# A fused attention and softplus layer on one core: the branch to the general path moved ahead of the last two units, and matmul steps unmixed

## The chip, the cores and the metric

The kernel runs on 1 core of one Trainium2 chip. The metric is device microseconds of one execution. Before the change three runs gave 687.23, 687.34 and 687.76 us; the median is 687.34 us.

## What is computed

The reference computes windowed attention with four sink keys (4 batches, 8 heads, 768 positions, head size 64, window 128), lays the heads side by side into x (3072 tokens x 512), and puts x through a layer with a softplus between two weight matrices:

```python
scores = scale * np.matmul(q, k.transpose(0, 1, 3, 2))
scores = np.where(is_sink | in_window, scores, -1000000000.0)
a = np.exp(scores - max); a = a / (a.sum + 1e-09)
x = (a @ v).transpose(0, 2, 1, 3).reshape(B * S, H * D)
h = x @ w_in                                      # 512 -> 2048
g = np.maximum(h, 0.0) + np.log1p(np.exp(-np.abs(h)))
return (g @ w_out).astype(np.float32)             # 2048 -> 512
```

The result has float32 accuracy. Each operand of the wide products is therefore kept as a rounded high part and a low remainder (`xh`/`xl`, `gh`/`gl`, and two planes of each weight), and a product is three matmuls: high by high, low by high, high by low.

## The kernel before

**Tiles.** The 3072 tokens are cut into 12 chunks of 256 (`CT`). The hidden width of 2048 is cut into 8 units of 256 (`FP`). For unit s of a chunk, `up(s)` makes `h` (128 partitions x 2 x 256) with 24 matmuls of 256 columns (line 574). `softplus(s)` runs Abs, Exp and Ln on ACT (lines 582 to 584). `gate(s)` adds the maximum on DVE (line 590) and rounds the result to `gh`, mostly on POOL (line 63). `residue(s)` makes `gl` on DVE (line 67). `down(s)` adds unit s into the two accumulators of the chunk with 12 matmuls of 512 columns (line 617); after unit 7 `store` copies both accumulators to SBUF, one on ACT and one on DVE, and SP stores them (line 629).

**Order.** `_fast` writes the order of all engines by hand. A string `START` gives the first stretch; then a loop over i runs one step per head, and each letter of a string in `STEADY` issues one piece of work for a unit or a head that lies a fixed distance from i. A step holds `up` of unit i-8, `softplus` and `gate` of that unit, `residue` of unit i-9, `down` of unit i-10 (units are counted through all chunks, 0 to 95), and the attention of one head: scores S (lines 263, 264), values V (lines 438, 444), and the work of the other engines between them. From i = 19 on (`MIXED`) the letters M and m issue `up` and `down` mixed: two up matmuls, one down matmul, and so on. For that `up` and `down` are generators that yield after each matmul, and `mixed` draws from them. Attention ends at i = 96; from then on a step is `up`, `down` and the work between. Step 103 has `up` of unit 95 and `down` of unit 93; steps 104 and 105 have the `down` of units 94 and 95 alone.

**The branch.** The fast path is valid only for some inputs. `_fast_flag` (line 817, issued at i = 100) reduces what was seen to one integer. When `_fast` is through, `values_load` (line 1003) loads it into a register on all five engines, and `tc.If(ok < 1)` (line 1004) enters `_general`, a complete second computation, when it is 0. With these inputs it is 1, so every engine jumps over the code of `_general`. Where the branch isn't taken, each engine runs a short block, also line 1004, that waits until the engine's own work so far is done and then raises the engine's semaphore by as much as `_general` would have. Later waits thus count the same on both paths. Before the change only the end of the program (line 1037) stands behind that block.

The two lines on which this hangs:

```python
        ok = nc.values_load(c.flag[:1, :1], min_val=0, max_val=1)
        with tc.If(ok < 1):
            _general(c)
```

Of the kernel before, what the change touches and what calls it, by code (L numbers as in the profile page):

```python
# [22 lines left out]
P = 128  # L23
# [446 lines left out]

def _weight_dma(c, s, k, half):

    src = c.a["w"][s, k, :, half * WH : (half + 1) * WH]
    tag = f"{WTAG[k]}{s}{half}"
    r = c.wp.tile([P, 4 * WH if c.w64 else 2 * WH], I16 if c.w64 else F32, tag=tag, name=f"{tag}r")
# [48 lines left out]
def _weight_high(c, e, eng):  # L528

    s, k, half = e  # L530
    n = (4, 2)[k]
    tag = f"{WTAG[k]}{s}{half}"
    c.w[e] = c.wp.tile([P, 2, n // 2, WC // n], F32R, tag=tag, name=tag)
    w, x = _weight_parts(c, e)
    _copy(c.nc, eng, w[:, 0], x)
# [20 lines left out]
class _Moe:  # L556
# [7 lines left out]
    def up(self, s):  # L564
        c, nc = self.c, self.c.nc
        xh, xl = c.x[self.chunk]
        if c.ps_h is None:
            c.ps_h = c.follow("ps_h")
        h = c.ps_h.tile([P, 2, CT], F32, tag="h", name=f"h{self.chunk}_{s}")
        prods = [(e, cc, j) for cc in range(4) for e in ("hh", "lh", "hl") for j in range(2)]  # L570
        for k, (e, cc, j) in enumerate(prods):
            wt = c.w[s, 0, cc // 2][:, "hl".index(e[0]), cc % 2, j * P : (j + 1) * P]
            x = (xh if e[1] == "h" else xl)[:, cc]
            nc.tensor.matmul(h[:, j], wt, x, start=k == 0, stop=k >= len(prods) - 2, skip_group_check=True)  # L574
            yield
        self.h[s] = h
# [25 lines left out]
    def down(self, s, *js):  # L602
        c, nc = self.c, self.c.nc
        if s == 0 and js[0] == 0:
            self.acc = [c.ps_acc.tile([P, DM], F32, tag=f"acc{t}", name=f"acc{self.chunk}_{t}") for t in range(CH)]
        gh, gl = self.g[s]
        prods = [(j, t, x, e) for x, e in ((gh, 0), (gh, 1), (gl, 0)) for j in js for t in range(CH)]
        if len(js) == 1:
            prods.sort(key=lambda p: p[1])
        else:  # L610
            prods[: 4 * len(js)] = sorted(prods[: 4 * len(js)], key=lambda p: p[:2])
        last = s == FP - 1 and js[-1] == 1
        for k, (j, t, x, e) in enumerate(prods):
            start = s == j == 0 and t not in [p[1] for p in prods[:k]]
            stop = last and t not in [p[1] for p in prods[k + 1 :]]
            w = c.w[s, 1, j][:, e, 0]
            nc.tensor.matmul(  # L617
                self.acc[t][:], x[:, j, t * P : t * P + P], w, start=start, stop=stop, skip_group_check=True
            )
            yield  # L620
        if last:
            self.store()

    def store(self):
        c, nc = self.c, self.c.nc
        for t, acc in enumerate(self.acc):
            o = c.stg.tile([P, DM], F32, tag="stg", name=f"o{self.chunk}_{t}")
            _copy(nc, c.E["out"][t], o[:], acc[:])
            nc.sync.dma_start(c.out[bass.ds(self.row + t * P, P), :], o[:])


def _fast(c):
# [57 lines left out]

    def products(i, name, k, *args):
        m, s = divmod(i, H)
        if not 0 <= i < n * H:
            return iter(())
        while any(e[:2] == (s, k) for _, e in todo["l"]):
            stage("l")(i)
        return getattr(moe[m], name)(s, *args)

    def dense(*args):
        return lambda i: list(products(i, *args))  # L700

    def mixed(rest):
        def run(i):
            done, live, rounds = object(), True, 6
            if not rest:
                c.mix = products(i, "up", 0), products(i - lag, "down", 1, 0, 1)
                if (i - lag) % H == 0:
                    rounds = 0
                    for _ in range(12):
                        next(c.mix[0], None)  # L710
            up, down = c.mix
            while live and (rest or rounds):
                rounds -= 1
                got = [next(p, done) for p in (up, up, down)]
                live = any(g is not done for g in got)

        return run
# [17 lines left out]
    def idle(k):  # L735
# [39 lines left out]
    with c.tc.manual_schedule():  # L775
# [15 lines left out]
        for i in range(2 * H + 1, (n + 1) * H + lag + 1):  # L791
            for part in "JjGLx" + c.STEADY[i >= c.MIXED][i % H == 0]:
                run, ahead = parts[part]
                run(i + ahead)
            if i >= 2 * H + lag and i % 2 == 0 and checks:
                _weight_check(c, *checks.pop(0))
            if i == n * H + lag:
                for e in checks:
                    _weight_check(c, *e)
                _fast_signs(c)  # L800
            if i == n * H + 2 * lag:
                _fast_flag(c)


# [54 lines left out]
def _general_masks(c):  # L859
# [7 lines left out]
    for i in range(NB):  # L867
# [58 lines left out]
def _general(c):  # L926

    tc, nc = c.tc, c.nc
    with ExitStack() as st:
        pool = lambda n, bufs: st.enter_context(tc.tile_pool(name=n, bufs=bufs))  # L930
        psum = lambda n, bufs: st.enter_context(tc.tile_pool(name=n, bufs=bufs, space=bass.MemoryType.PSUM))
        c.stg, c.gp, c.xp, c.mp = pool("gstg", 2), pool("gp", 1), pool("gxp", 1), pool("gmp", 1)
        c.ps_acc, c.ps_h, c.gs, c.gt, c.gx = psum("gacc", 1), psum("gh", 1), psum("gs", 1), psum("gt", 1), psum("gx", 1)
        _general_weights(c)
        keep = _general_masks(c)
        with tc.For_i(0, B, 1) as b:
            for n in range(NCH):
                xh, xl = c.x[n] = [c.xp.tile([P, 4, CT], F32R, tag=f"x{e}", name=f"gx{e}{n}") for e in "hl"]
                for h in range(H):
                    if h % 2 == 0:  # L940
                        xt = c.gx.tile([P, CT], F32, name=f"g_x{n}_{h}", tag="g_x")
                    _general_head(c, b, n, h, keep, xt)
                    if h % 2 == 1:
                        _copy(nc, "A", xh[:, h // 2], xt[:])
                        _sub(nc, "V", xl[:, h // 2], xt[:], xh[:, h // 2])
                m = _Moe(c, n)
                m.row = b * S + n * CT
                for s in range(FP):
                    list(m.up(s))
                    m.softplus(s)  # L950
                    m.gate(s)
                    m.residue(s)
                    for j in range(2):
                        list(m.down(s, j))


def _kernel(tc, a, out):
# [3 lines left out]
    c.E = dict(qkh="A", ql="V", kl="V", vh="A", vl="P", xh="A", xl="P", gl="V", tl="P", out="AV")  # L961
    c.x, c.vs, c.vsr, c.vsh = {}, {}, {}, {}
    c.w64 = a["w"].dtype == mybir.dt.int64
    nc.scalar.preload_act_table_set("natural_log_exp_and_others")
    with ExitStack() as keep:
# [10 lines left out]
        ones = c.room[:].rearrange("p a b -> p (a b)").unsqueeze(1).broadcast_to([P, CT // 64, 64])  # L976
        _zero(nc, c.sk[:].rearrange("p (a b) -> p a b", b=64), ones)
        with ExitStack() as st:
            pool = lambda n, bufs: st.enter_context(tc.tile_pool(name=n, bufs=bufs))
            psum = lambda n, bufs: st.enter_context(tc.tile_pool(name=n, bufs=bufs, space=bass.MemoryType.PSUM))  # L980
# [3 lines left out]
            c.ps_acc, c.ps_t, c.ps_x = psum("ps_acc", 1), psum("ps_t", 1), psum("ps_x", 1)  # L984
            fronts = {}
# [15 lines left out]
            with tc.manual_schedule(engines=ORDERED):  # L1001
                _fast(c)
# [13 lines left out]
Ctx.WL = "PPPVVPPVPPVVVPVPVPPVVVPPVPPVVPPV"  # L1016
Ctx.MIXED = 19
# [62 lines left out]
```

## Time and profile before

| | |
|---|---|
| median of 3 runs | 687.34 us (687.23 to 687.76) |
| the profiled execution | 686.84 us |
| its span, first to last instruction | 685.1 us |
| PE busy | 664.3 us (97% of the span), 4319 matmuls |
| DVE, ACT, POOL busy | 542.1, 477.9, 446.8 us (79, 70, 65%) |
| chain that ended last | PE 83% of the span |

The span is the time between the first and the last instruction of the program; 1.7 us of the execution lie around it. The page cuts the span into 40 slices: PE is at 9 tenths in nearly all of them, and DMA falls to almost nothing in the last five. The chain that ended last is followed back from the last instruction: `acc` of line 617 and `h` of line 574 are 36% of the span each.

### The profile page before, as it was taken

What the parts mean: (1) busy time and instruction counts of PE and PEld (TensorE: products, weight loads), DVE (VectorE), ACT (ScalarE), POOL (GpSimd) and SP (SyncE); (2) the same over time, 40 slices, a digit from 0 to 9 for tenths busy, and PEclk for the clock granted to TensorE, in tenths of its full rate; (3) what the DMA queues carried; (4) which work ended last, traced back from release to release, by engine and by line L of the source; (5) the groups of instructions that cost most, each with busy time, mean ns of one, the idle gap of its engine ahead of it and who ended that gap; (6) DMA issues with size and microseconds to landing.
All of it is one profiled execution on the core that took longest, in us unless ns stands there. A gap on an engine that the chain in (4) does not pass through costs nothing.

```text
span 685.1 us, 14176 instructions
## 1 busy us (share of the span) xinstructions
PE 664.3 (97%) x4319; PEld 592.2 (86%) x4319; DVE 542.1 (79%) x1461; ACT 477.9 (70%) x1213; POOL 446.8 (65%) x817
## 2 busy tenths in 40 slices
PE   5999989999999999999999999999999999999995
PEld 3588878999999999999999999999999999999984
DVE  6899977878888888888889888888878888753332
ACT  6999866768677677767777776777777777753331
POOL 7675479678667776795776775786866776762110
PEclk9999999999999999999999999999999999999998
DMA  8996334344344435344444434433443434310001
GB/s 311 351 404 203 103 89 126 87 116 121 102 121 125 113 90 149 97 107 117 114 117 117 125 91 110 137 107 97 131 118 92 141 93 119 100 51 1 32 1 36
DMA packets 97656, 83.33 MB, mean 122 GB/s; under 512 B 51876, under 2 KB 79140, under 8 KB 97572
## 3 DMA queue, kind: packets, MB, share of 16 engines
q1 hardware_dynamic: 97428, 82.35, 41.7%
q8 instruction: 36, 0.59, 0.4%
q14 instruction: 48, 0.39, 0.2%
q10 hardware_dynamic: 144, 0.00, 0.0%
HBM read 65.53 MB, written 16.78 MB: 120 GB/s over the span
## 4 chain that ended last, share of the span: by engine, by line
PE 83%; POOL 0%; ACT 0%; DVE 0%; POOLq 0%; issue 0%
PE acc L617 36%; PE h L574 36%; PE x L444 5%; PE s L264 3%; PE s L263 3%; PE x L438 1%; PE ts L334 0%; POOL wo L67 0%; DVE mt L590 0%; DVE o L61 0%; ACT mt L583 0%; ACT mt L584 0%; ACT mt L582 0%; POOLq L1003 0%; POOL pt L409 0%; POOL pt L406 0%
## 5 line engine op out<-in xcount | busy, mean ns | idle before, releaser
L574 PE MATMUL h<-xh,wi 128*128 128x256 f32 x1536 | 298.2, 282 | 0.3 <-DVE mt L590 0.3
L574 PEld LDWEIGHTS h<-xh,wi 128*128 128x128 f32 x1536 | 269.1, 189 | 30.1 <-issue 1.1
L617 PE MATMUL acc<-wo,gh 128*128 128x512 f32 x768 | 292.5, 395 | 1.8 <-POOL wo L67 1.2
L574 PE MATMUL h<-xl,wi 128*128 128x256 f32 x768 | 152.9, 281 | 0.0
L574 PEld LDWEIGHTS h<-xl,wi 128*128 128x128 f32 x768 | 140.2, 188 | 14.0
L617 PEld LDWEIGHTS acc<-wo,gh 128*128 128x128 f32 x768 | 143.2, 188 | 5.6 <-POOL wo L67 1.5
L617 PE MATMUL acc<-wo,gl 128*128 128x512 f32 x384 | 145.1, 393 | 1.3 <-DVE gl L67 1.3
L63 POOL TENSOR_SCALAR gh<-mt 128x512 fp32r<-128x512 f32 x88 | 54.8, 623 | 133.5 <-DVE mt L590 104.2
L582 ACT ACTIVATE mt<-h 128x512 f32<-128x512 f32 x96 | 57.6, 600 | 106.7 <-PE h L574 106.0
L590 DVE SCALAR_TENSOR_TENSOR mt<-h,mt 128x512 f32<-128x512 f32 x96 | 65.5, 683 | 35.9 <-ACT mt L584 35.9
L67 POOL TENSOR_TENSOR tl<-u,th 128x256 f32<-128x256 f32 x80 | 64.2, 802 | 45.2 <-issue 32.2
L293 ACT ACTIVATE a<-a,stats 128x136 f32<-128x136 f32 x192 | 76.0, 397 | 7.2 <-DVE stats L292 6.7
L617 PEld LDWEIGHTS acc<-wo,gl 128*128 128x128 f32 x384 | 72.3, 188 | 5.5 <-DVE gl L67 2.2
L67 DVE TENSOR_TENSOR kl<-qk,qkh 128x400 fp32r<-128x400 f32 x80 | 73.3, 916 | 2.5
L67 DVE TENSOR_TENSOR gl<-mt,gh 128x512 fp32r<-128x512 f32 x96 | 71.6, 746 | 4.1 <-POOL gh L63 4.1
L67 DVE TENSOR_TENSOR qkh<-qk,qkh 64x256 fp32r<-64x256 f32 x80 | 44.8, 560 | 27.8 <-ACT qkh L59 21.8
L318 POOL TENSOR_SCALAR a<-a,rc 128x128 f32<-128x128 f32 x156 | 58.1, 385 | 7.5 <-DVE rc L307 7.5
L583 ACT ACTIVATE mt<-mt 128x512 f32<-128x512 f32 x96 | 60.8, 633 | 3.0
L584 ACT ACTIVATE mt<-mt 128x512 f32<-128x512 f32 x96 | 60.7, 633 | 3.1
L59 ACT CAST qkh<-qk 128x656 fp32r<-128x656 f32 x80 | 59.1, 739 | 1.4 <-DMA qk<-qk 1.0
L406 POOL TENSOR_SCALAR_AFFINE_SELECT pt<-th 128x256 fp32r<-128x256 f32 x80 | 50.3, 628 | 0.0
L444 PE MATMUL x<-pt,vv 128*128 128x256 f32 (+1 forms) x216 | 47.6, 323 | 0.0
(191 smaller groups left out, 1098.2 us busy)
## 6 DMA issues: line engine op xcount, KB each, us to landing
qk<-qk SPq DMA_DIRECT2D x160, 164.0 KB, 3.1
rows<-xf SPq DMA_DIRECT2D x320, 32.0 KB, 1.6
u<-rows SPq DMA_DIRECT2D x80, 128.0 KB, 2.7
vr<-v SPq DMA_DIRECT2D x32, 192.0 KB, 2.8
out<-o SPq DMA_DIRECT2D x24, 256.0 KB, 2.3
qk<-qk SPq DMA_DIRECT2D x8, 328.0 KB, 5.7
vr<-v SPq DMA_DIRECT2D x16, 128.0 KB, 2.3
wi00r<-w SPq DMA_DIRECT2D x1, 511.8 KB, 5.8
```

The lines of the kernel that those rows point to most:

```text
L59: nc.scalar.copy(out, in_)
L63: nc.gpsimd.tensor_scalar(out, in_, 1.0, 0.0, ALU.mult, ALU.add)
L67: (nc.vector if eng == "V" else nc.gpsimd).tensor_tensor(out, a, b, ALU.subtract)
L293: nc.scalar.activation(a, a, AF.Exp, bias=nm, scale=-1.0, accum_out=total)
L318: (nc.vector if eng == "V" else nc.gpsimd).tensor_scalar(a, a, rc[:, j : j + 1], 0.0, ALU.mult, ALU.add)
L444: nc.tensor.matmul(x[:, :, o], w, pt[:, :, m], start=False, stop=n == 2, skip_group_check=True)
L574: nc.tensor.matmul(h[:, j], wt, x, start=k == 0, stop=k >= len(prods) - 2, skip_group_check=True)
L582: nc.scalar.activation(t[:], h[:], AF.Abs)
L583: nc.scalar.activation(t[:], t[:], AF.Exp, scale=-1.0)
L584: nc.scalar.activation(t[:], t[:], AF.Ln, bias=1.0)
L590: nc.vector.scalar_tensor_tensor(t[:], h[:], 0.0, t[:], ALU.max, ALU.add)
L617: nc.tensor.matmul(self.acc[t][:], x[:, j, t * P : t * P + P], w, start=start, stop=stop, skip_group_check=True)
```

## The change

1. **The branch stands earlier.** The steps leave out `softplus`, `gate`, `residue` and `down` of units 94 and 95 (the last two units of the last chunk). `values_load` and `If` follow the `up` of unit 95 and the `down` of unit 93. Behind the `If`, on both paths, the new function `_tail` does what was left out. `_general` now ends with the `up` of those two units into the same PSUM tiles (`held_h`) and with the same accumulators (`held_acc`). `_tail` takes its SBUF tiles from two new pools.
2. **The end.** In the tail the `down` of unit 95 finishes accumulator 0 first and then accumulator 1. The copy of accumulator 1 is cut into two halves, ACT taking the left and DVE the right.
3. **Equal products.** `mixed` goes; `up` and `down` are plain functions, and a step from i = 19 on (`JOINED`) runs the 24 matmuls of `up` in one piece and the 12 of `down` in one piece. The order of letters in the two `STEADY` strings is new: `up`, then `softplus` at once, scores, later `down`, values.

```diff
@@ _fast
+    def dense(name, k, *args):
         def run(i):
...
+            m, s = divmod(i, H)
+            if 0 <= i < n * H:
+                while any(e[:2] == (s, k) for _, e in todo["l"]):
+                    stage("l")(i)
+                getattr(moe[m], name)(s, *args)
...
-            for part in "JjGLx" + c.STEADY[i >= c.MIXED][i % H == 0]:
+            for part in "JjGLx" + c.STEADY[i >= c.JOINED][i % H == 0]:
                 run, ahead = parts[part]
-                run(i + ahead)
+                if not (part in "FPRB" and i + ahead >= (n - 1) * H + FP - 2):
+                    run(i + ahead)
@@ down, store
+        if last and c.tail:
+            prods.sort(key=lambda p: p[1])
...
+            if t and c.tail:
+                _copy(nc, "A", o[:, : DM // 2], acc[:, : DM // 2])
+                _copy(nc, "V", o[:, DM // 2 :], acc[:, DM // 2 :])
+            else:
+                _copy(nc, c.E["out"][t], o[:], acc[:])
@@ new
+def _tail(m):
+    for s in (FP - 2, FP - 1):
+        m.softplus(s)
+        m.gate(s)
+        m.residue(s)
+    for s in (FP - 2, FP - 1):
+        m.down(s, 0, 1)
@@ _kernel
         ok = nc.values_load(c.flag[:1, :1], min_val=0, max_val=1)
+        c.held_h, c.held_acc = [m.h[s] for s in (FP - 2, FP - 1)], m.acc
         with tc.If(ok < 1):
             _general(c)
+        c.tail = True
+        with ExitStack() as st:
+            c.mp, c.stg = (st.enter_context(tc.tile_pool(name=n, bufs=2)) for n in ("tmp", "tstg"))
+            with tc.manual_schedule(engines=ORDERED):
+                _tail(m)
@@ tables
 Ctx.STEADY = (
     ("kWUqYpKSFTXRDVPONE", "SWTkpUKERDNFXPqYVO"),
-    ("MYKqpmXWFSTRPNVnO", "qMSKpYWmXFTVRPONn"),
+    ("UKpFWSTRXPqNBVOYn", "WSpUKFTqBXVORPNnY"),
 )
```

PE, the last matmuls of the mixed steps and what follows, before (`h_7` is unit 95, `acc` with `gh_5`/`gl_5`, `gh_6` and `gh_7` are the down of units 93, 94 and 95):

```order
2863 L574 MATMUL h_7_9927<-xh_8992,wi_1170 128x256 x2
2864 L617 MATMUL acc_0_9689<-wo_1109,gl_5_9922 128x512
2865 L574 MATMUL h_7_9927<-xl_8993,wi_1170 128x256 x2
2866 L617 MATMUL acc_1_9690<-wo_1109,gl_5_9922 128x512
2867 L617 MATMUL acc_0_9689<-wo_1191,gh_6_9925 128x512 x2
```

PE at the same place in the changed program, up to the jump:

```order
2207 L575 MATMUL h_7_9920<-xh_8987,wi_1170 128x256 x4
2208 L575 MATMUL h_7_9920<-xl_8988,wi_1170 128x256 x2
2209 L619 MATMUL acc_0_9708<-wo_1018,gh_5_9867 128x512 x2
2215 L619 MATMUL acc_0_9708<-wo_1109,gl_5_9906 128x512
2216 L619 MATMUL acc_1_9709<-wo_1109,gl_5_9906 128x512
2217 L1015 TENSOR_LOAD flag_i
2218 L1017 COMPARE_AND_BRANCH
```

The mixed rows have become two runs of equal rows, and the load of the flag and the branch stand where the down of unit 94 stood; the 24 down matmuls of units 94 and 95 follow behind the branch.

ACT, from the softplus of unit 94 to the branch, before:

```order
919 L582 ACTIVATE mt_6_9918<-h_6_9881 128x512 [waits DVE_49,PE_49]
920 L583 ACTIVATE mt_6_9918<-mt_6_9918 128x512 [waits Activation_49]
921 L584 ACTIVATE mt_6_9918<-mt_6_9918 128x512 [waits Activation_49]
922 L582 ACTIVATE mt_7_9964<-h_7_9927 128x512 [waits DVE_49,PE_49]
926 L1003 TENSOR_LOAD flag_i [waits DVE_49]
927 L1004 COMPARE_AND_BRANCH
```

ACT in the changed program: the last row of the fast part, the branch, and the tail:

```order
918 L584 ACTIVATE mt_5_9860<-mt_5_9860 128x512 [waits Activation_49]
919 L1015 TENSOR_LOAD flag_i [waits DVE_49]
920 L1017 COMPARE_AND_BRANCH
1168 L582 ACTIVATE mt_6_13864<-h_6_9881 128x512 [waits DMAHW2_49,DMAHW3_49,DMAHW1_49,DMAHW4_49,DMAHW0_49,DMAHW5_49,DVE_49,DMAHW6_49,PE_49,DMAHW7_49,Activation_49,Pool_49]
1169 L582 ACTIVATE mt_7_13873<-h_7_9920 128x512 [waits DVE_49,PE_49]
1170 L583 ACTIVATE mt_6_13864<-mt_6_13864 128x512 [waits Activation_49]
1171 L583 ACTIVATE mt_7_13873<-mt_7_13873 128x512 [waits Activation_49]
1172 L584 ACTIVATE mt_6_13864<-mt_6_13864 128x512 [waits Activation_49]
```

The branch now stands behind unit 93, the two units of the tail take turns on ACT, and the first Abs of the tail waits for every engine and every DMA queue, where it waited for PE and DVE alone.

## Rows read from the trace of the kernel before

**Rows 1.** Groups of instructions, 115 to 672 us: busy us, mean ns | idle before.

```profile
L574 PE MATMUL h<-xh,wi 128*128 128x256 f32 x1358 | 269.1, 282 | 0.0
```

**Rows 2.** Timeline of PE, a mixed step: its first product, and what follows its last.

```profile
408.12 0.40 PE L574 MATMUL h<-xh,wi 128*128 128x256 f32 x2
...
413.76 0.28 PE L263 MATMUL s<-qkh 128*128 128x264 f32 x1
```

**Rows 3.** Timeline of PE, an up in one piece (73.63 to 75.77: 18 matmuls).

```profile
73.63 0.63 PE L574 MATMUL h<-xh,wi 128*128 128x256 f32 x4
...
75.77 0.64 PE L574 MATMUL h<-xh,wi 128*128 128x256 f32 x4
```

**Rows 4.** Timeline of PE from the end of the mixed steps on.

```profile
672.20 1.98 PE L617 MATMUL acc<-wo,gh 128*128 128x512 f32 x8
674.01 1.07 PE L617 MATMUL acc<-wo,gl 128*128 128x512 f32 x4
675.64 2.11 PE L617 MATMUL acc<-wo,gh 128*128 128x512 f32 x8 [0.56 <-POOL gh L63]
677.59 1.07 PE L617 MATMUL acc<-wo,gl 128*128 128x512 f32 x4
```

**Rows 5.** Timeline of ACT and DVE in the same stretch.

```profile
672.16 0.60 ACT L582 ACTIVATE mt<-h 128x512 f32<-128x512 f32 x1 [3.67 <-PE h L574]
...
673.46 0.63 ACT L584 ACTIVATE mt<-mt 128x512 f32<-128x512 f32 x1
...
674.12 0.69 DVE L590 SCALAR_TENSOR_TENSOR mt<-h,mt 128x512 f32<-128x512 f32 x1 [3.41 <-ACT mt L584]
...
678.47 0.59 ACT L59 COPY o<-acc 128x512 f32<-128x512 f32 x1 [4.38 <-PE acc L617]
678.70 0.69 DVE L61 COPY o<-acc 128x512 f32<-128x512 f32 x1 [2.38 <-PE acc L617]
```

**Rows 6.** Lines 1003 and 1004, the branch: duration in ns, first to last start in us.

```profile
L1003 PEldq TENSOR_LOAD <-flag_i x1: 487/487/487, 676.4 to 676.4; - x1
...
L1004 SPq EVENT_SEMAPHORE  x8: 17/17/17, 683.2 to 683.8; - x8
...
L1004 PEldq COMPARE_BRANCH  x1: 3902/3902/3902, 677.0 to 677.0; - x1
...
L1004 SPq COMPARE_BRANCH  x1: 45/45/45, 679.9 to 679.9; - x1
L1004 PEldq EVENT_SEMAPHORE  x1: 51/51/51, 680.9 to 680.9; - x1
```

**Rows 7.** Line 438 (first matmul of V), one step: PE's sequencer, then the matmul.

```profile
L438 PEldq EVENT_SEMAPHORE  x1: 51/51/51, 131.4 to 131.4; - x1
...
L438 PE MATMUL x<-sk,vs x1: 285/285/285, 134.0 to 134.0; 128*128 128x256 f32 x1
```

**Rows 8.** Busy time by stretch (us, PE, PEld, DVE, ACT, POOL, PEclk, DMA share, GB/s).

```profile
131.40:134.00 2.60, 2.60 (x19) 2.39 (x19) 2.54 (x4) 0.74 (x2) 2.60 (x5) 1.00 0.53 159
679.00:680.70 1.70, 0.00 (x0) 0.00 (x0) 0.39 (x1) 0.06 (x1) 0.00 (x0) 1.00 0.48 169
680.90:685.00 4.10, 0.00 (x0) 0.00 (x0) 0.00 (x0) 0.00 (x0) 0.00 (x0) 0.50 0.18 57
```

**Rows 9.** Timeline of PE near the start.

```profile
16.07 1.09 PE L354 MATMUL t<-ident,a 128*128 128x128 f32 x4 [0.75 <-POOL wi L63]
...
18.27 1.22 PE L419 MATMUL x<-sk,vsf 128*128 128x256 f32 x2
...
22.07 0.66 PE L354 MATMUL t<-ident,a 128*128 128x128 f32 x4
```

**Rows 10.** Landing of the stores of `out`: all 24 (median), and the last two.

```profile
out<-o SPq DMA_DIRECT2D x24, 256.0 KB, 2.3
...
DMA to landing us min/median/max: 3.2/3.2/3.2
```

**Rows 11.** Line 1037, the end of the program, on SP.

```profile
L1037 SPq EVENT_SEMAPHORE  x10: 17/28/28, 683.8 to 685.1; - x10
```

More of the change, by code (lines that the diff above doesn't have):

```diff
@@ L468, in out, with _weight_dma @@
             _sub(nc, "V" if h == H - 1 else c.E["xl"], xl[:, h // 2], xf, xh[:, h // 2])
-def _weight_dma(c, s, k, half):
+def _weight_dma(c, s, k, half, pool=None):
     src = c.a["w"][s, k, :, half * WH : (half + 1) * WH]
     tag = f"{WTAG[k]}{s}{half}"
-    r = c.wp.tile([P, 4 * WH if c.w64 else 2 * WH], I16 if c.w64 else F32, tag=tag, name=f"{tag}r")
+    r = (pool or c.wp).tile([P, 4 * WH if c.w64 else 2 * WH], I16 if c.w64 else F32, tag="raw" if pool else tag, name=f"{tag}r")
     if c.w64:
@@ L532, in _weight_high @@
     tag = f"{WTAG[k]}{s}{half}"
-    c.w[e] = c.wp.tile([P, 2, n // 2, WC // n], F32R, tag=tag, name=tag)
+    if e not in c.w:
+        c.w[e] = c.wp.tile([P, 2, n // 2, WC // n], F32R, tag=tag, name=tag)
     w, x = _weight_parts(c, e)
@@ L568, in up @@
             c.ps_h = c.follow("ps_h")
-        h = c.ps_h.tile([P, 2, CT], F32, tag="h", name=f"h{self.chunk}_{s}")
+        h = c.held_h[s % 2] if c.held_h else c.ps_h.tile([P, 2, CT], F32, tag="h", name=f"h{self.chunk}_{s}")
         prods = [(e, cc, j) for cc in range(4) for e in ("hh", "lh", "hl") for j in range(2)]
@@ L604, in down @@
         if s == 0 and js[0] == 0:
-            self.acc = [c.ps_acc.tile([P, DM], F32, tag=f"acc{t}", name=f"acc{self.chunk}_{t}") for t in range(CH)]
+            self.acc = c.held_acc or [c.ps_acc.tile([P, DM], F32, tag=f"acc{t}", name=f"acc{self.chunk}_{t}") for t in range(CH)]
         gh, gl = self.g[s]
@@ L689, in stage @@
         return run
[L691 to L702, printed above, removed]
-        def run(i):
[L704 to L715, printed above, removed]
+    def dense(name, k, *args):
+        def run(i):
+            m, s = divmod(i, H)
[3 more added lines that the diff above has]
+                getattr(moe[m], name)(s, *args)
         return run
@@ L758, in _fast @@
         "U": (dense("up", 0), -H),
-        "M": (mixed(False), -H),
-        "m": (mixed(True), -H),
+        "B": (dense("down", 1, 0, 1), -H - lag),
         "F": (call(moe, "softplus"), -H),
@@ L802, in _fast @@
                 _fast_flag(c)
+    return moe[-1]
 def _fast_signs(c):
@@ L836, in _general_weights @@
     for e in ((s, k, half) for s in range(FP) for k in range(2) for half in range(2)):
-        _weight_dma(c, *e)
+        _weight_dma(c, *e, c.gp)
         r = c.raw[e]
@@ L932, in _general @@
         c.stg, c.gp, c.xp, c.mp = pool("gstg", 2), pool("gp", 1), pool("gxp", 1), pool("gmp", 1)
-        c.ps_acc, c.ps_h, c.gs, c.gt, c.gx = psum("gacc", 1), psum("gh", 1), psum("gs", 1), psum("gt", 1), psum("gx", 1)
+        c.gs, c.gt, c.gx = psum("gs", 1), psum("gt", 1), psum("gx", 1)
         _general_weights(c)
         keep = _general_masks(c)
+        for n in range(NCH):
+            c.x[n] = [c.xp.tile([P, 4, CT], F32R, tag=f"x{e}{n}", name=f"gx{e}{n}") for e in "hl"]
         with tc.For_i(0, B, 1) as b:
             for n in range(NCH):
-                xh, xl = c.x[n] = [c.xp.tile([P, 4, CT], F32R, tag=f"x{e}", name=f"gx{e}{n}") for e in "hl"]
+                xh, xl = c.x[n]
                 for h in range(H):
@@ L948, in _general @@
                 for s in range(FP):
-                    list(m.up(s))
+                    m.up(s)
                     m.softplus(s)
@@ L953, in _general @@
                     for j in range(2):
-                        list(m.down(s, j))
+                        m.down(s, j)
+        m = _Moe(c, NCH - 1)
+        for s in range(FP):
+            m.up(s)
+            if s < FP - 2:
+                m.softplus(s)
+                m.gate(s)
+                m.residue(s)
+                m.down(s, 0, 1)
 def _kernel(tc, a, out):
@@ L962, in _kernel @@
     c.x, c.vs, c.vsr, c.vsh = {}, {}, {}, {}
+    c.held_h, c.held_acc, c.tail = None, None, False
     c.w64 = a["w"].dtype == mybir.dt.int64
@@ L977, in _kernel @@
         _zero(nc, c.sk[:].rearrange("p (a b) -> p a b", b=64), ones)
+        c.ps_acc = keep.enter_context(tc.tile_pool(name="ps_acc", bufs=1, space=bass.MemoryType.PSUM))
         with ExitStack() as st:
             pool = lambda n, bufs: st.enter_context(tc.tile_pool(name=n, bufs=bufs))
-            psum = lambda n, bufs: st.enter_context(tc.tile_pool(name=n, bufs=bufs, space=bass.MemoryType.PSUM))
+            psum = lambda n, bufs: st.enter_context(
+                tc.tile_pool(name=n, bufs=bufs, space=bass.MemoryType.PSUM, side="right")
+            )
             c.xp, c.mp, c.stg = pool("xp", 2), pool("mp", 2), pool("stg", 4)
@@ L993, in follow @@
                 fronts[name].close()
-                return scores_pool(name, 2, st)
+                return scores_pool(name, 2, st if name == "ps_s" else keep)
             for n in ("ps_s", "ps_h"):
@@ L1016 @@
 Ctx.WL = "PPPVVPPVPPVVVPVPVPPVVVPPVPPVVPPV"
-Ctx.MIXED = 19
+Ctx.JOINED = 19
 Ctx.STEADY = (
     ("kWUqYpKSFTXRDVPONE", "SWTkpUKERDNFXPqYVO"),
-    ("MYKqpmXWFSTRPNVnO", "qMSKpYWmXFTVRPONn"),
+    ("UKpFWSTRXPqNBVOYn", "WSpUKFTqBXVORPNnY"),
 )
```

7 lines of the change are left out of this document (2 added, 5 removed).

## The prediction

> **What bounds the kernel now.** I read three views in turn. The groups of instructions say that from 115 to 672 us PE never waits: its largest group, 1358 up matmuls, has 0.0 us of idle time before it [rows 1]. So in the steps the time is PE's own pace, and DVE, ACT and POOL, a fifth to a third of the span idle, cost nothing as long as none of them is late. The timeline of PE gives the pace: the 24 up and 12 down matmuls of one mixed step take 413.76 - 408.12 = 5.64 us [rows 2], and where an up ran in one piece 18 matmuls took 2.14 us, 0.119 each [rows 3]. Third, the end. I set E = 672.20 us, where the first down matmul behind the mixed steps starts; eight of these take 674.01 - 672.20 = 1.81 us, 0.226 each [rows 4]. The down of unit 94 runs under the softplus of unit 95. Then PE waits 0.56 us, does the down of unit 95, and ends at 677.59 + 1.07 = 678.66. The two accumulators are out of PSUM at 679.39 [rows 5]. Only then comes the branch on SP: compare at 679.9, next instruction at 683.2, a jump of 3.3 us in which the last stores land [rows 6]. The span ends at 685.1, which is E + 12.9.
>
> **What the change moves in the steps.** Per step: 24 x 0.119 + 12 x 0.226 = 5.57 us, with one changeover more or less 5.60, against 5.64 [rows 2 to 4]. Over the 85 steps from i = 19 on that would be -3.4 us. The pieces were read where they ran alone, and each new piece starts a little slower, so the other end is 0; I take half, **-1.7 us**. No work is added in the steps. The moved softplus makes ACT wait until the up is through, with the weights' cast, the exponentials and the copy of x queued behind it; in steps with a sink transpose the cast of the next keys waits too. All of it is wanted by PE half a step to a step later, and the 0.0 us [rows 1] says there is room; if the room were gone, one lateness per chunk would be paid by PE. On SP the row stores now stand ahead of the output stores that wait for copies, which can only help. The flag's few small DVE operations stay where they were.
>
> **What it moves at the end, from E on.** In the changed program the jump comes before the last two units, and the tail can start only behind it: its first Abs waits for PE's semaphore at a value that PE reaches only by the raise in the block behind its own jump, and this block first waits for all of PE's matmuls. The same holds for DVE, POOL and SP, but these are through early: their last work belongs to unit 93, more than ten us before E, and their jumps lie under PE's work. If that cover were gone, each would cost the 3.3 us that SP showed [rows 6]. PE's own jump is not covered:
>
> - *PE's jump.* PE's sequencer runs ahead of the array: it dealt with the wait of a V at 131.4, whose matmul started at 134.0 [rows 7], and that stretch holds 19 matmuls, two of them under way at its start [rows 8]; so 17 ahead. Seventeen back from E are 12 down and 5 up: 12 x 0.226 + 5 x 0.119 = 3.3 us. From the flag's load to the compare it is 0.6 us, from the compare to the block 680.9 - 677.0 = 3.9 us [rows 6]. The raise falls at E - 3.3 + 0.6 + 3.9 = E + 1.2. Bounds: E + 0.1, since the block waits for the last matmul, and E + 2.3, as far behind PE's end as it was before (680.9 - 678.66).
> [...]
> - *The softplus in the open.* ACT starts 0.1 us later. Abs and Exp take 673.46 - 672.16 = 1.30 us, Ln 0.66 to DVE's start [rows 5]. The two units take turns on ACT, so unit 94 is through after Abs, Abs, Exp, Exp, Ln: 2 x 1.30 + 0.66 = 3.3 us. DVE starts at E + 4.6.
> - From DVE's start through POOL to PE it was 675.64 - 674.12 = 1.5 us [rows 4, 5]: PE resumes at **E + 6.1**. Unit 95 follows in time on all three engines.
> - *24 down matmuls in a row.* 12 x 0.226 = 2.7, then the last twelve with their tail 2.9 (672.20 to 675.08) [rows 4]: E + 11.7 at full clock.
> - *The clock.* PE rests 5.9 us, from E + 0.2 to E + 6.1. [...] I take 3.8 us at half pace: 1.9 us lost, E + 13.6. Ends: 0, and all 24 on the lower level, 24 x 0.226 = 5.4 us.
> - *Copies.* Accumulator 0 is copied under the last six matmuls. Accumulator 1 goes in two halves, which don't overlap because both write one tile and DVE waits for ACT: half of 0.59 and half of 0.69 [rows 5] and a start between them, 0.8 us, where it was 0.73. With 0.1 us to the store's issue: E + 14.5.
> - *Landing.* 2.3 us is the median of all stores, 3.2 us the last two took [rows 10]; I take 2.8: E + 17.3.
> - *The end.* From its first instruction on SP to the last it is 685.1 - 683.8 = 1.3 us [rows 11]; some of the waits pass while the store is under way, so 1.1: **E + 18.4**.
>
> So the end is 18.4 - 12.9 = 5.5 us longer. In short: the jump leaves the last store's path (PE's end to the span's end was 6.5 us and becomes 4.8), but the softplus of unit 94 and the down of unit 94 come out of their cover, and PE starts slow. Less the steps: 5.5 - 1.7 = **+3.8 us**. This is reckoned within one execution of 686.84 us, with 1.7 us around its span, which I leave unchanged; the median of the three runs is 0.5 us above it, and I add to the median: 687.34 + 3.8 = 691.1 us.
>
> **Rivals.**
> - *The tail is not held (faster).* If the softplus of 94 and 95 ran under the last up and down, as the move suggests, PE would wait for its jump alone: E + 1.2 + 5.6 + 0.8 + 0.1 + 2.8 + 1.1 = E + 11.6, which is -1.3, with the steps -3.0: 684.3 us. Against it stands PE's raise, which the first Abs must see. With the clock kept, it decides at a start of PE before E + 4.2: earlier is a gain. 7%.
> - *The jump ends under the matmuls and the clock holds (no change).* Then the raise is at E + 0.1 and nothing is lost to the clock: 3.8 - 1.1 - 1.9 = +0.8, 688.1 us. For it: the clock was held for 2.1 us before it fell, and the sequencer may run further ahead than the 17 of [rows 8]. Against it: PE would still rest 4.8 us. 10%. [...]
> - *The clock stays low through all 24.* 5.4 in place of 1.9: +7.3, 694.6 us. [...] 12%.
> - *A new wait in the steps.* The up of a chunk's first unit now follows the scores at once, and its last products need the last head's x: 0.48 us of scores and 22 x 0.119 = 2.6 us of up after the V, 3.1 us for the copy, the two additions, the cast and the remainder, where the mixed order left longer. If it were 0.3 us late in each of 11 chunks: +3.3, 694.4 us. 7%.
>
> **How the numbers follow.** The likeliest is the sum as it stands, 64%, 691.1 us; its own range, with the bounds of the jump, the landing and the steps, is 689.0 to 693.5. The first rival leaves 7% below, and the clock and the new wait reach to 694.6; the range 687.9 to 694.8 leaves out the first rival and the far ends of the others. A measurement can tell about 0.2% (1.4 us) from no change: faster is the first rival, 0.07; the same is the second and the low end of the sum, 0.13; slower 0.80.
>
> **What would show it.** On ACT the Abs of unit 94 should start 1 to 2.5 us after the last down of unit 93 and right behind PE's semaphore of line 1017; the Abs of 95 should follow it directly. PE should then stand still for 5 to 7 us, with POOL named as the releaser. The clock row behind the pause should show 0.50, and the first tail matmuls some 0.45 us apart, the last ones 0.23. SP's jump should lie far ahead of the end, and the last store should be followed by the end within 4.5 us. PE should have 0.0 us of idle time from 115 us to E, and E should come 0 to 3.4 us sooner than 672.20. I am wrong if an Abs of the tail runs before PE's last down of unit 93 has ended, if PE's pause is under 4 us, or if E itself moves by more than 4 us.

## The result, and the profile after

The changed kernel takes 691.25 us (median of 6 runs, 690.52 to 691.88) against 687.20 us for the kernel before (6 runs, 686.86 to 687.76): a ratio of 1.0059, with a 95% interval of 1.0046 to 1.0072, or 4.05 us more. The forecast was 691.1. The profiled execution took 691.18 us with a span of 689.5 us.

First the steps. The groups of instructions of PE, 115 to 672 us, and under it the timeline of PE through one step of the changed kernel:

```profile
L575 PE MATMUL h<-xh,wi 128*128 128x256 f32 x1359 | 218.2, 283 | 0.0
```

```profile
408.38 0.64 PE L575 MATMUL h<-xh,wi 128*128 128x256 f32 x4
...
411.26 0.29 PE L263 MATMUL s<-qkh 128*128 128x264 f32 x1
...
411.75 2.00 PE L619 MATMUL acc<-wo,gh 128*128 128x512 f32 x8
...
414.50 0.28 PE L438 MATMUL x<-sk,vs 128*128 128x256 f32 x1
```

PE still waits for nobody. The up takes 411.26 - 408.38 = 2.88 us and the down 414.50 - 411.75 = 2.75, together 5.63 us, where the mixed block took 5.64 [rows 2]. The equal products gave nothing here. (The busy time of the group, 218.2 us where it was 269.1 [rows 1], is no gain: in one piece four up matmuls are busy for 0.64 us together, with a mean of 283 ns each, so that their overlap lies within the group. The mean was 282 ns before.) The same comes out over nearly all of the steps: one product V, in the kernel before and then in the changed kernel, starts at

```profile
127.37 0.28 PE L438 MATMUL x<-sk,vs 128*128 128x256 f32 x1
```

```profile
127.55 0.28 PE L438 MATMUL x<-sk,vs 128*128 128x256 f32 x1
```

and from there to E (below) it is 672.20 - 127.37 = 544.8 us before and 672.31 - 127.55 = 544.8 us after.

Then the end. The timeline of PE, and that of ACT and DVE in the same stretch:

```profile
669.60 2.00 PE L619 MATMUL acc<-wo,gh 128*128 128x512 f32 x8
671.44 1.07 PE L619 MATMUL acc<-wo,gl 128*128 128x512 f32 x4
...
677.57 3.78 PE L619 MATMUL acc<-wo,gh 128*128 128x512 f32 x8 [5.07 <-POOL gh L63]
...
684.92 0.61 PE L619 MATMUL acc<-wo,gl 128*128 128x512 f32 x2
```

```profile
673.39 1.09 ACT L582 ACTIVATE mt<-h 128x512 f32<-128x512 f32 x2 [12.90 <-PEq L1017]
...
675.40 1.15 ACT L584 ACTIVATE mt<-mt 128x512 f32<-128x512 f32 x2
676.12 1.29 DVE L590 SCALAR_TENSOR_TENSOR mt<-h,mt 128x512 f32<-128x512 f32 x2 [13.40 <-ACT mt L584]
...
685.57 0.37 ACT L59 COPY o<-acc 128x256 f32<-128x256 f32 x1 [0.78 <-PE acc L619]
685.98 0.42 DVE L61 COPY o<-acc 128x256 f32<-128x256 f32 x1 [6.72 <-ACT o L59]
```

The first two rows are the down of unit 93. Its twelve matmuls at 0.226 us put E, where the next down matmul would have started, at 669.60 + 2.71 = 672.31 (672.20 before, [rows 4]). In its place PE stands still for 5.07 us. ACT has waited 12.90 us for an event of PE's sequencer on line 1017, the block behind the untaken branch; nothing of the softplus of units 94 and 95 runs before that. This wait is called the hold below. The next two fences have the load of the flag on PE, and the branch with who waited for it (duration in ns, first to last start in us):

```profile
L1015 PEldq TENSOR_LOAD <-flag_i x1: 487/487/487, 668.9 to 668.9; - x1
```

```profile
L1017 ACTq COMPARE_BRANCH  x1: 50/50/50, 660.4 to 660.4; - x1
...
L1017 ACTq EVENT_SEMAPHORE  x1: 17/17/17, 663.0 to 663.0; - x1
...
L1017 PEldq COMPARE_BRANCH  x1: 3632/3632/3632, 669.5 to 669.5; - x1
L1017 PEldq EVENT_SEMAPHORE  x1: 51/51/51, 673.2 to 673.2; - x1
...
  ACT mt L582: 12.9, 1
```

ACT's jump (2.6 us, from 660.4 to 663.0) lies under PE's work and costs nothing. PE loads the flag at 668.9, 3.4 us before E, compares at 669.5, and raises its semaphore at 673.2, 0.7 us after its last matmul has ended (671.44 + 1.07 = 672.51). What the clock did, by stretch (us, PE, PEld, DVE, ACT, POOL, PEclk, DMA share, GB/s):

```profile
672.50:675.00 2.50, 0.01 (x1) 0.00 (x0) 0.00 (x0) 1.61 (x4) 0.00 (x0) 1.00 0.02 7
...
675.50:676.00 0.50, 0.00 (x0) 0.00 (x0) 0.00 (x0) 0.50 (x3) 0.00 (x0) 0.50 0.00 0
...
677.60:682.00 4.40, 4.40 (x10) 3.48 (x11) 1.65 (x2) 0.00 (x0) 0.51 (x1) 0.50 0.00 0
...
682.50:685.50 3.00, 3.00 (x14) 2.13 (x12) 0.00 (x0) 0.59 (x1) 0.00 (x0) 1.00 0.00 0
```

The granted clock falls to 0.50 while PE rests and is still there when PE resumes: ten matmuls fall in the first 4.4 us, at 0.50, and fourteen in the last 3.0, at 1.00. The 24 down matmuls take 684.92 + 0.61 - 677.57 = 7.96 us.

### The profile page after: what moved, and what is told of

It reads as the page before. It is cut to its first block, busy times and chain, and to the rows that moved or that the text cites. A ratio compares the mean times of both kernels' runs of the same rounds, so it can differ in the third digit from the quotient of the medians.

```text
span 689.5 us, 14213 instructions
## 1 busy us (share of the span) xinstructions
PE 665.6 (97%) x4319; PEld 596.6 (87%) x4319; DVE 523.5 (76%) x1461; ACT 474.2 (69%) x1214; POOL 434.6 (63%) x817
## 5 line engine op out<-in xcount | busy, mean ns | idle before, releaser
L575 PE MATMUL h<-xh,wi 128*128 128x256 f32 x1536 | 247.0, 283 | 0.3 <-DVE mt L590 0.3
L575 PEld LDWEIGHTS h<-xh,wi 128*128 128x128 f32 x1536 | 211.6, 191 | 4.9 <-issue 0.9
L619 PE MATMUL acc<-wo,gh 128*128 128x512 f32 x768 | 200.1, 397 | 6.3 <-POOL gh L63 5.1
L619 PEld LDWEIGHTS acc<-wo,gh 128*128 128x128 f32 x768 | 138.9, 190 | 32.0 <-POOL gh L63 5.5
L67 POOL TENSOR_TENSOR tl<-u,th 128x256 f32<-128x256 f32 x80 | 70.1, 876 | 131.8 <-issue 125.1
L575 PEld LDWEIGHTS h<-xl,wi 128*128 128x128 f32 x768 | 119.7, 192 | 0.0
L619 PE MATMUL acc<-wo,gl 128*128 128x512 f32 x384 | 108.3, 392 | 1.3 <-DVE gl L67 1.3
L318 POOL TENSOR_SCALAR a<-a,rc 128x128 f32<-128x128 f32 x156 | 64.9, 428 | 2.5 <-DVE rc L307 2.5
L464 DVE TENSOR_TENSOR xt<-x,xt 64x256 f32<-64x256 f32 x80 | 33.0, 412 | 31.0 <-ACT xt L59 30.9
L67 DVE TENSOR_TENSOR kl<-qk,qkh 128x400 fp32r<-128x400 f32 x80 | 53.4, 668 | 2.3
```

What stands on the lines that cost most here:

```text
L67: (nc.vector if eng == "V" else nc.gpsimd).tensor_tensor(out, a, b, ALU.subtract)
L318: (nc.vector if eng == "V" else nc.gpsimd).tensor_scalar(a, a, rc[:, j : j + 1], 0.0, ALU.mult, ALU.add)
L619: nc.tensor.matmul(self.acc[t][:], x[:, j, t * P : t * P + P], w, start=start, stop=stop, skip_group_check=True)
```

## Experiments

Each ratio is to the kernel before, timed in the same job; its medians there were 686.97 (experiments 1 to 4) and 687.07 us (5 to 8). Differences are between medians. The change was timed in an earlier job, in which the kernel before took 687.20 us, so a difference from the change carries some 0.2 us of that. In every program E is 2.71 us after the start of the down of unit 93, if nothing else is said.

**1. The equal products alone.** The kernel before with the new order of letters and plain `up` and `down`, the branch at the end:

```diff
-    ("MYKqpmXWFSTRPNVnO", "qMSKpYWmXFTVRPONn"),
+    ("UKpFWSTRXPqNBVOYn", "WSpUKFTqBXVORPNnY"),
```

> Equal products alone: the branch stays at the end. Theory (read from the changed kernel's trace, where an up in one piece takes 2.88 us and a down 2.75, together 5.63 against 5.64 mixed): no change, 0.0 +- 0.4 us against before; the first down of unit 94 starts within 0.3 us of 672.20. Rival (the prediction's term): 1.7 us faster, up to 3.4.

686.42 us against 686.97: ratio 0.9990 (0.9981 to 0.9999), 0.55 us less. That is just past the 0.4 us of the expectation. The timeline of PE from the down of unit 94 on:

```profile
671.95 1.98 PE L616 MATMUL acc<-wo,gh 128*128 128x512 f32 x8
...
674.67 1.98 PE L616 MATMUL acc<-wo,gh 128*128 128x512 f32 x8
676.49 1.07 PE L616 MATMUL acc<-wo,gl 128*128 128x512 f32 x4
```

The down of unit 94 starts at 671.95, within 0.3 us of before, and the product V of 127.37 at 127.15, so the steps between take 544.8 us as before: they give nothing, as expected from the trace after and against the prediction's -1.7. What is gained is at the end: the softplus now follows its up at once, and PE's 0.56 us before the down of unit 95 [rows 4] is gone; PE ends 1.1 us earlier (678.66 before, 677.56 here), 0.25 of it E. In the profiled run, of 687.00 us, that was lost again: the two stores took 2.39 us to issue (677.98 to 680.37), where they take 0.81 before and in experiment 6. Why isn't known.

**2. The branch and the tail alone.** The changed kernel with the mixed steps of before:

```diff
-    ("UKpFWSTRXPqNBVOYn", "WSpUKFTqBXVORPNnY"),
+    ("MYKqpmXWFSTRPNVnO", "qMSKpYWmXFTVRPONn"),
```

> The early branch and the tail alone, the steps mixed as before. Theory: all of the loss is behind E, so +4.0 us against before (3.5 to 4.6), and the end from E on is as long as in the whole change, 17.2 us. Rival (the prediction's sum): +5.5 us, which the equal products then bring down by 1.7.

691.68 us: ratio 1.0072 (1.0058 to 1.0085), 4.7 us more, just above the 3.5 to 4.6 expected. PE, and its clock in the first of its last 24 matmuls (columns as above):

```profile
672.39 0.40 PE L620 MATMUL acc<-wo,gl 128*128 128x512 f32 x1
678.21 3.61 PE L620 MATMUL acc<-wo,gh 128*128 128x512 f32 x8 [5.42 <-POOL gh L63]
```

```profile
678.20:681.40 3.20, 3.19 (x8) 2.51 (x9) 1.70 (x2) 0.00 (x0) 0.56 (x1) 0.50 0.00 0
```

The last down of unit 93 starts at 672.39, so E is 672.62, and the span of 689.5 us ends at E + 16.9, where 17.2 was expected. PE rests 0.35 us longer than in the change, but its clock is back after 3.2 us of work, where it took 4.7, and the 24 matmuls take 7.28 us. All of the loss belongs to the branch and its tail; the 0.4 us between the medians of this version and of the change is no more than the two profiled executions differ by in the clock alone.

**3. The tail in an else block.** The tail becomes the other side of the same branch, and the general path finishes its own outputs again, so that the tail reads nothing that the general path writes:

```diff
-        with tc.If(ok < 1):
+        with tc.If(ok < 1) as general:
             _general(c)
         c.tail = True
-        with ExitStack() as st:
+        with general.Else(), ExitStack() as st:
```

> The tail stands in an else block of the same branch, and the general path again finishes its own outputs, so nothing in the tail reads what the general path writes. Theory (the hold behind PE's raise costs, not the jump): Abs of unit 94 runs under PE's last up and down, PE rests about 1 us for its own jump and resumes at E + 1.1, the clock stays at 1.00, 24 down take 5.6 us, copies 0.9, landing and end 3.1: E + 10.7 against E + 12.9 before, so 2.2 us faster than before and 6.3 faster than the change. Rival (every engine's jump lies on the path, whatever waits for what): PE rests 4 us or more and the kernel is no faster than before.

684.70 us (684.62 to 684.95): ratio 0.9966 (0.9954 to 0.9978), 2.3 us less than before, and 6.55 less than the change. PE's branch, the timeline at the same place, and PE by stretch:

```profile
L1009 PEldq COMPARE_BRANCH  x1: 3692/3692/3692, 669.1 to 669.1; - x1
```

```profile
669.45 0.60 ACT L582 ACTIVATE mt<-h 128x512 f32<-128x512 f32 x1 [4.96 <-PE h L575]
...
673.34 2.08 PE L619 MATMUL acc<-wo,gh 128*128 128x512 f32 x8 [1.18 <-POOL gh L63]
```

```profile
673.40:679.00 5.60, 5.60 (x24) 4.33 (x24) 1.51 (x2) 0.59 (x1) 0.38 (x1) 1.00 0.01 3
```

PE's jump is as long as in the change (3.69 us), but the Abs of unit 95 waits only for `h` and runs under the down of unit 93. PE rests 1.18 us in place of 5.07, the clock stays at 1.00, and the 24 down matmuls take 5.6 us. So the hold was the cost, and not the jump, which is the same. The jump was over at 669.1 + 3.7 = 672.8; the last 0.5 us PE waited for `gh` of unit 94, because ACT did the Abs of 95 before the Exp of 94.

**4. Matmuls in the pause.** The changed kernel, with 16 matmuls between the jump and the down of unit 94 whose products nobody reads:

```diff
+    fill = c.fill.tile([P, DM], F32, name="fill")
+    for _ in range(16):
+        c.nc.tensor.matmul(fill[:], c.sk[:, :P], c.w[0, 1, 0][:, 0, 0], start=True, stop=True, skip_group_check=True)
```

> The changed kernel with 16 extra matmuls of 512 columns into an unused PSUM bank, issued on PE between the jump and the down of unit 94 (their products are read by nobody). Theory (the clock's fall in the pause costs 2.4 us): the extra matmuls run from E + 0.9 to E + 4.6, the clock stays at 1.00, the 24 down take 5.6 us in place of 7.96: 2.3 us faster than the change, 1.8 slower than before. Rival (PE's slow pace behind the pause has another cause): no gain, or as much loss as the extra matmuls overrun the softplus.

688.56 us: ratio 1.0023 (1.0014 to 1.0032), 2.7 us less than the change. PE, and its clock in the last 24:

```profile
673.06 3.90 PE L878 MATMUL fill<-wo,sk 128*128 128x512 f32 x16 [0.95 <-PEq L1021]
...
677.19 2.11 PE L619 MATMUL acc<-wo,gh 128*128 128x512 f32 x8 [0.23 <-POOL gh L63]
```

```profile
677.20:682.90 5.70, 5.70 (x24) 4.42 (x24) 1.68 (x2) 0.59 (x1) 0.53 (x1) 1.00 0.00 0
```

The softplus lies in the open as before, but PE's last 24 matmuls run at a granted clock of 1.00: 5.7 us in place of 7.96. PE waits as long for the softplus as in the change (it resumes at E + 5.3 in both), so this prices the clock's part of that execution at 2.3 us; the other 0.4 is a down of unit 93 that starts at 669.20 in place of 669.60. The price isn't a fixed one. In the four programs in which PE rests for 4.7 to 5.4 us (the change, experiments 2, 5 and 6) the granted clock was back after 4.7, 3.2, 5.1 and 5.8 us of work, and the 24 matmuls took 7.96, 7.28, 8.09 and 8.46 us: 1.6 to 2.8 us more than here.

**5. A short body.** The general path is cut to seven instructions, so that the jump goes a few instructions ahead; its results are left out:

```diff
-        _general_weights(c)
-        keep = _general_masks(c)
...
+        for s, h in enumerate(c.held_h):
+            for j in range(2):
+                nc.tensor.matmul(h[:, j], c.w[s, 0, 0][:, 0, 0, :P], c.sk[:], start=j == 0, stop=True, skip_group_check=True)
```

> The changed kernel with the general path cut down to seven instructions (four matmuls into the two held h tiles, one copy each on ACT and DVE, one operation on POOL), so that the untaken branch skips a few instructions instead of a whole second computation; the general path's results are left out. Theory (the jump is slow because its target is far): PE's branch takes well under 1 us in place of 3.63, PE's raise falls at E + 0.1 to 0.3 in place of E + 0.9, and the rest of the end is as in the change, so 0.7 us faster than the change: 690.5. Rival (an untaken branch takes this long whatever it skips): 3.6 us again and no gain.

691.61 us: ratio 1.0065 (1.0051 to 1.0078), no faster than the change. The branch, and PE around it:

```profile
L990 ACTq COMPARE_BRANCH  x1: 45/45/45, 661.0 to 661.0; - x1
L990 ACTq EVENT_SEMAPHORE  x1: 17/17/17, 661.2 to 661.2; - x1
...
L990 PEldq COMPARE_BRANCH  x1: 223/223/223, 670.1 to 670.1; - x1
L990 PEldq EVENT_SEMAPHORE  x1: 51/51/51, 673.2 to 673.2; - x1
```

```profile
672.08 1.07 PE L619 MATMUL acc<-wo,gl 128*128 128x512 f32 x4
673.70 1.08 ACT L582 ACTIVATE mt<-h 128x512 f32<-128x512 f32 x2 [12.57 <-PEq L990]
...
677.87 3.78 PE L619 MATMUL acc<-wo,gh 128*128 128x512 f32 x8 [4.72 <-POOL gh L63]
```

On the jump the theory holds: PE's takes 0.22 us in place of 3.63, and ACT's 0.2 in place of 2.6 (to its next instruction), so it was the large body that made the jump slow in the change. What the jump waited for there isn't shown. One trace of it is in the DMA queues: while PE jumps in the change, 669.5 to 673.2 us, the only packet that moves is one of 0.02 MB on the queue that the profile calls `instruction` (packets, MB, share of 16 engines):

```profile
q8 instruction: 1, 0.02, 2.1%
```

There is one such packet under PE's jump in each of the nine programs with the far target, and none here from 668 to 673.5 us. In the change it has moved by 670.5, though, and the jump ends at 673.2. PE's raise now follows the end of its last matmul (672.08 + 1.07 = 673.15) at once. On the time it fails: PE's pause is only 0.35 us shorter (4.72), since ACT starts 0.5 us behind the raise where it was 0.2, and the 24 matmuls start at a granted clock of 0.50 again, for 5.1 us of work. And this program's down of unit 93 starts at 670.24 where the change's starts at 669.60; all of that delay is there already at 128 us (the product V that starts at 127.55 in the change starts at 128.19). Where it comes from isn't settled. From E (672.95) on, the end takes 689.9 - 672.95 = 16.95 us in place of 17.2; by the pause, the far jump itself costs the change 0.35 us.

**6. The end of before.** The changed kernel with the down of unit 95 alternating between the accumulators, and both copied whole:

```diff
-        if last and c.tail:
-            prods.sort(key=lambda p: p[1])
...
-            if t and c.tail:
-                _copy(nc, "A", o[:, : DM // 2], acc[:, : DM // 2])
-                _copy(nc, "V", o[:, DM // 2 :], acc[:, DM // 2 :])
-            else:
-                _copy(nc, c.E["out"][t], o[:], acc[:])
+            _copy(nc, c.E["out"][t], o[:], acc[:])
```

> The changed kernel with the end of before: the down of unit 95 alternates between the accumulators, and both are copied whole, one on ACT and one on DVE. Theory (the early copy of accumulator 0 lets the last store go alone): both stores are issued within 0.5 us behind PE's end, the last one lands 3.2 us after its issue in place of 2.0, and the end comes 1.0 to 1.4 us later than in the change: 692.4. Rival (two copies at once and two stores at once cost nothing): copies 0.73 in place of 0.87, so 0.1 us faster than the change.

690.92 us (690.00 to 691.52): ratio 1.0053 (1.0040 to 1.0067). Against the change that is no difference that the runs can tell. The down of unit 93, the last 24 matmuls and the stores:

```profile
669.09 2.00 PE L617 MATMUL acc<-wo,gh 128*128 128x512 f32 x8
...
677.09 3.78 PE L617 MATMUL acc<-wo,gh 128*128 128x512 f32 x8 [5.10 <-POOL gh L63]
...
684.47 1.08 PE L617 MATMUL acc<-wo,gl 128*128 128x512 f32 x4
...
686.02 0.81 SPq L628 DMA_DIRECT2D out<-o  x2
```

Both stores are issued by 686.83, and the span ends at 689.8, 3.0 us later (in the change 2.7, from 686.76 to 689.5). The 3.2 us that the last two stores of before took to land [rows 10] don't come back; the expectation rested on them. They had landed while the far jumps of four engines were under way (over at 680.9 on PE, 681.8 on ACT, 682.8 on DVE, 683.2 on SP), but nothing here separates that from other causes. This program's down of unit 93 starts half a microsecond earlier than the change's, so from E on its end is longer after all: its 24 matmuls take 684.47 + 1.08 - 677.09 = 8.5 us, 0.5 more, and the stores 0.3 more. The 0.5 is the clock, which stays low for 5.8 us of work in place of 4.7. So part 2 of the change is worth 0.3 us at most by itself, a quarter of what was expected.

**7. The else version in order.** ACT finishes unit 94 before unit 95, and accumulator 1 is copied whole by ACT:

```diff
-                _copy(nc, "A", o[:, : DM // 2], acc[:, : DM // 2])
-                _copy(nc, "V", o[:, DM // 2 :], acc[:, DM // 2 :])
+            _copy(nc, "A" if c.tail else c.E["out"][t], o[:], acc[:])
...
-            with tc.manual_schedule(engines=ORDERED):
+            with tc.manual_schedule(engines=ORDERED | {mybir.EngineType.Activation}):
```

> The tail in an else block, and two small things more: ACT does the softplus of unit 94 to its end before that of 95, and accumulator 1 is copied whole by ACT (0.59 us) in place of two halves one after the other (0.87). Theory (in the else version PE's last wait was for gh of unit 94, 0.39 us after its jump had ended, because the Abs of 95 stood before the Exp of 94): PE resumes as soon as its jump ends, E + 0.7, 0.4 us earlier, and the last store is issued another 0.25 us earlier: 0.6 us faster than the else version, 684.1. Rival (the jump ends late enough to take it all): 0.25 us.

683.89 us: ratio 0.9953 (0.9939 to 0.9967), 0.8 us less than experiment 3. PE's branch, the rounding of unit 94 on POOL, and PE:

```profile
L1005 PEldq COMPARE_BRANCH  x1: 3789/3789/3789, 669.0 to 669.0; - x1
```

```profile
669.18 0.62 POOL L63 TENSOR_SCALAR gh<-mt 128x512 fp32r<-128x512 f32 x1 [7.69 <-PE h L575]
...
672.96 2.06 PE L619 MATMUL acc<-wo,gh 128*128 128x512 f32 x8 [0.94 <-POOL gh L63]
```

PE rests 0.94 us. The row names POOL, but `gh` of unit 94 had been done at 669.8; the jump ends at 669.0 + 3.8 = 672.8, and that is what PE waits for now. From E (671.82) PE resumes 0.24 us earlier than in experiment 3, where 0.4 was expected, since the jump ends at E + 1.0 and not at E + 0.7; the span ends at E + 10.6 in place of E + 11.0.

**8. One unit in the else block.** Only unit 95 is left to it, and the flag is loaded one step ahead:

```diff
-                if not (part in "FPRB" and i + ahead >= (n - 1) * H + FP - 2):
+                if not (part in "FPRB" and i + ahead == n * H - 1):
...
+            if i == n * H + 2 * lag + 3:
+                c.ok = c.nc.values_load(c.flag[:1, :1], min_val=0, max_val=1)
```

> As the version before it, but only unit 95 is left to the else block, and the flag is loaded before the down of unit 94. So 24 down matmuls stand in front of PE's branch in place of 12 down and 12 up, and the 0.5 us of the load are out of the way. Theory (PE's sequencer runs about 17 matmuls ahead: 17 x 0.226 = 3.8 us of down against a jump of 3.7): PE's pause shrinks from 0.7 us to 0.1 or less, 0.7 us faster than the version before it, 683.4. Rival (unit 95's softplus, behind ACT's, DVE's and POOL's jumps, comes too late): PE waits for gh of unit 95 and nothing is gained, or some lost.

682.89 us (682.83 to 683.26): ratio 0.9939 (0.9926 to 0.9953), 4.2 us less than before and 8.4 less than the change. It is the fastest version found. PE's branch and PE:

```profile
L1005 PEldq COMPARE_BRANCH  x1: 3818/3818/3818, 670.5 to 670.5; - x1
```

```profile
671.79 1.98 PE L619 MATMUL acc<-wo,gh 128*128 128x512 f32 x8
...
674.51 1.09 PE L619 MATMUL acc<-wo,gh 128*128 128x512 f32 x4
```

The jump runs from 670.5 to 674.3, all of it under the 12 down matmuls of unit 94 and the end of those of unit 93, and the down of unit 95 starts at 674.51, twelve matmuls of 0.227 us after that of unit 94, with no idle time. From the first down of unit 94 to the end of the span it is 681.1 - 671.79 = 9.3 us, where it was 12.9; the other 0.4 us of the gain in span is an earlier E.

## Why the prediction was right, step by step

The number was right (691.1 against 691.25), and so was the mechanism: the hold, the softplus and the down of unit 94 in the open, the fall of the clock, and no jump behind the last store. That the number came so close is luck. The steps were taken 1.8 us too short, and the end from E on 1.2 us too long: 0.3 on PE's raise, 0.6 on the softplus and 0.9 on landing and end too long, 0.5 on the clock and 0.1 on small pieces too short. Times are from E, 672.31 in the profile after; the last column is read from the rows above.

| step | forecast | measured |
|---|---|---|
| the steps before E | -1.7 us | +0.1 us |
| PE's raise | E + 1.2 | E + 0.9 |
| DVE starts the gate of 94 | E + 4.6 | E + 3.8 |
| PE resumes | E + 6.1 | E + 5.3 |
| 24 down matmuls | 7.5 us | 7.96 us |
| PE ends | E + 13.6 | E + 13.2 |
| the copies end | E + 14.4 | E + 14.1 |
| end of the span | E + 18.4 | E + 17.2 |

- **The steps: wrong.** "Over the 85 steps from i = 19 on that would be -3.4 us ... I take half, -1.7 us". The step took 5.63 us, not 5.60, and E came 0.1 us later, where "0 to 3.4 us sooner" was named as a sign; from the product V at 127 us to E both kernels took 544.8 us. The pace of 0.119 and 0.226 us was read from pieces that ran alone; in the steps an up matmul takes 0.120 and a down matmul 0.229 us. A difference of 0.04 us out of 5.6, read from a few rows and multiplied by 85, was no evidence. The other end that the prediction kept, 0, was the right value, and experiment 1 agrees.
- **The hold: right.** ACT waited for PE's sequencer on line 1017, and the Abs of unit 94 started 0.9 us after the last down of unit 93 had ended, just below the 1 to 2.5 us named. Experiment 3 shows that the hold is the cost: with the same jump and no hold, 6.55 us come back. The forecast counted the load at E - 3.3, from 17 matmuls; it was at E - 3.4. In experiment 8 the branch was handled 674.51 - 670.5 = 4.0 us ahead of PE's next matmul, again some 17 down matmuls at 0.227.
- **The jump: right, and its price small.** 3.63 us on PE, of which 0.7 showed behind PE's last matmul. With the near target of experiment 5 it was 0.22 us, while the far targets took 3.3 to 3.9 us on PE (3.33 in experiment 2, 3.90 before).
- **The softplus: mis-sized by 0.6 us.** Abs and Exp were charged as 1.30 us for each unit, the time of two that depend on each other. Where the two units take turns, the next instruction starts before the last has ended (the first Exp at 674.37, where the second Abs ends at 673.39 + 1.09 = 674.48): from the first Abs to the first Ln it was 675.40 - 673.39 = 2.0 us, not 2.6.
- **The clock: right in kind, 0.5 us too small.** It fell in the pause, as it had behind PE's end before [rows 8], and cost 2.3 us (experiment 4), where 1.9 had been taken. No run shows the 3.8 us at half pace behind that 1.9. They were the author's estimate, as long as the time from 18.27 to 22.07 [rows 9], where matmuls were slow: four transposes took 1.09 us at 16.07 and 0.66 at 22.07. The granted clock of that stretch was 1.00, so the slowness there isn't shown to be the clock's:

```profile
18.30:21.90 3.60, 3.60 (x16) 1.74 (x14) 3.23 (x10) 3.05 (x13) 3.52 (x5) 1.00 1.05 393
```

In the four programs in which PE rested for 4.7 to 5.4 us the clock stayed at 0.50 through 3.2 to 5.8 us of work, and that cost 1.6 to 2.8 us (experiment 4). So the size of this term was luck as well.
- **Landing and end: mis-sized by 0.9 us.** From the copies' end to the span's end the forecast had 18.4 - 14.4 = 4.0 us, and it was 689.5 - 686.4 = 3.1. The landing of 3.2 us, to which the estimate of 2.8 leaned, was that of the end of before: experiment 6 issues the two stores in the same way, and from there to the end of the span it is 3.0 us in all.
- **The rivals.** The tail that is not held was the wrong one for this kernel, but its 684.3 us is near what the else block measured (684.70). That is luck in part too: its sum has the same -1.7 for the steps, and from E on it gives 11.6 us where the else block took 11.0. A clock at 0.50 through all 24, a clock that holds, and a new wait in the steps did not occur.

Where the loss comes from, in the two profiled executions (the medians differ by 4.05 us): the softplus of unit 94 and PE's jump in the open, 5.07 us of rest in place of 0.56; 2.3 us of clock; less 2.6 us, because no jump stands behind the last store any more (3.1 us from the copies' end to the end of the span, where it was 685.1 - 679.4 = 5.7 [rows 5]; with the end of before in experiment 6 it is 689.8 - 686.3 = 3.5, so 0.4 of it are part 2, which its longer copies cut to 0.3). That makes 4.2 us; with 0.1 for E and 0.1 for longer copies it is the 4.4 us by which the span grew.

## What to carry to other kernels

In this kernel work behind the join of a branch waited for every engine that could have written its inputs on the other path, though the branch wasn't taken: ACT for 12.90 us, until PE's raise. Before moving a branch ahead of work that was hidden, look for what the first instruction behind it waits for, or put the work into an else block, where that wait didn't arise here. In experiment 8 the 3.8 us of the far jump on TensorE were hidden under the matmuls ahead of it, some 17 of 0.227 us: put such a jump behind as many of the long ones as it lasts, and load its flag earlier. A per-step gain of under one per cent, read from a handful of rows, should be entered as nothing.

## What the runs showed that was not expected

- The same untaken branch took PE 3.3 to 3.9 us with a far target and 0.22 us with a near one.
- The granted clock stayed at 1.00 for at least 2.5 us into PE's rest in the change (672.5 to 675.0) and for 5.3 us in experiment 2 (672.8 to 678.1). After PE resumed it was 0.50 through 4.4 us of matmuls without a pause in the change, and through 3.2 to 5.8 us from program to program. In experiment 4 a rest of 0.95 us, and in experiment 3 one of 1.18, did not lower it.
- With the same work ahead of the steps, E differed by over a microsecond between the profiled executions: the down of unit 93 started at 669.04 in experiment 8, at 669.60 in the change and at 670.24 in experiment 5. From the product V at 127 us to E all ten programs take 544.8 to 545.0 us, so the difference arises before 127 us. Each program has one profile, and the runs of one program spread as far (690.52 to 691.88 us in the change), so it isn't shown that the program makes it. Small differences between medians of different programs must be read with that in mind; the terms above are therefore taken from E.
